# Two attention accumulators, and four PSUM banks shared in time, in a fused pooling-attention and mixture-of-depths kernel

## The chip, the core and the metric

The kernel runs on one core of a Trainium2 chip. The metric is the device time of one execution in microseconds (us), lower is better. The engines are called PE (TensorE, the matmuls), DVE (VectorE), ACT (ScalarE), POOL (GpSimd) and SP (SyncE, which here only issues DMAs). Each engine works through its own instructions in the order in which the program lists them, and waits on semaphores for the others. All arithmetic is fp32 unless said otherwise.

## What is computed

```python
# attention: B, H, S, D = 8, 8, 576, 64; keys and values are averaged over groups of 8 rows
k_p = k.reshape(B, H, Sp, pool, D).mean(axis=3)          # Sp = 72
v_p = v.reshape(B, H, Sp, pool, D).mean(axis=3)
scores = scale * np.matmul(q, k_p.transpose(0, 1, 3, 2))
attn = np.exp(scores - max); attn = attn / (attn.sum(-1) + 1e-09)
x = np.matmul(attn, v_p)                                  # to (B, S, 512)
# mixture of depths: 128 of 576 rows of each batch go through a small network
scores = np.einsum('bsd,d->bs', x, w_gate)
out = x.copy()
for b in range(B):
    top_idx = np.argpartition(-scores[b], capacity)[:capacity]   # capacity = 128
    xe = x[b, top_idx]
    ye = np.maximum(xe @ w1, 0.0) @ w2                    # 512 -> 1024 -> 512
    g = 1.0 / (1.0 + np.exp(-scores[b, top_idx]))
    out[b, top_idx] = x[b, top_idx] + g[:, None] * ye
```

## The kernel before

The kernel is one long program with its order written out by hand: nothing is rescheduled, and each engine executes its part of the list in that order. The names below are functions of the kernel; a line such as L232 is a line of it.

The 576 rows of a batch are cut into six chunks of 96 rows, so there are 48 chunks `a` in the whole program. Two chunks make a unit `u` (24 units, three a batch).

Attention, per unit and chunk:

- `pool_k` and `pool_v` add up groups of eight rows of k and v, on POOL for all batches but the first; `k_trans` and `q_trans` transpose on DVE; `gate_v` (L194) appends to the pooled v a column for the gate's score, beside a column of constants which gives the sum of the exponentials.
- `scores(u)` (L216) makes 16 matmuls, which use the PE array in four groups of 32 rows, into the PSUM tile `pS` (four banks). One ACT instruction of 72 x 1536 elements (L220) takes the exponential of all of it into `et`.
- `attend(a)` (L232) makes eight matmuls, one a head, into the PSUM tile `pA` (two banks, one buffer).
- `norm(a)` reads the sum of the exponentials and the gate's column from `pA` on ACT (L244, L245), inverts the sum on DVE (L247) and multiplies the rows by it into `xs` (L248).
- `store_x(u)` writes two chunks to the output in HBM; ACT's queue issues it.

The mixture of depths, for each batch after its attention, spread over the steps of the following batches:

- `score` adds the heads' gate scores (DVE), and POOL splits them into three bf16 numbers each. `row_bcast` (L293, L295) spreads the scores along rows with PE transposes and ACT copies, in two halves. `count` (L305 to L309) counts on DVE for each row how many have a higher score, `one_hot` (L316) makes a selection matrix of that, and `gather` (L323) multiplies it with indices and scores, whereupon POOL issues an indirect DMA that fetches the 128 chosen rows from the output in HBM (`xr`); it waits for the batch's stores.
- `gate` computes the sigmoid, `x_trans` (L346, L348) transposes the chosen rows, `hidden` (L358, L361) is the first product with its Relu, `finish` (L368, L373) the second, with the gate, the addition of the row, and an indirect DMA that scatters the rows to the output.

The PSUM of eight banks is divided like this: `pS` four, `pA` two, `pM` one (`row_bcast`, `gather`, `x_trans` and `hidden`, one after the other), `pF` one (`finish`).

The order comes from a main loop over chunks and a table of jobs. `at(a, slot, job)` puts a job into one of four slots of the step of chunk `a`; the loop runs slot 0, then `attend` and `norm` of the chunk, slot 1, in even steps `scores(u + 1)` and `q_trans(u + 2)`, and slots 2 and 3. The pieces of `hidden` and `finish` are spread over slots 1 and 2, so that they stand between `attend` and `scores` on PE:

```python
        for n, f in enumerate((0, 1, 2, 3, 4, 5, 8, 6, 7, 9, 10, 11, 12, 13, 14, 15)):
            c = (0, 0, 1, 1, 2, 2, 2, 3, 3, 3, 4, 4, 4, 5, 5, 5)[n]
            slot = (1, 2, 1, 2, 1, 2, 2, 1, 2, 2, 1, 2, 2, 1, 2, 2)[n]
            at(e + 8 + c, slot, *((hidden, b, f) if f < 8 else (finish, b, f - 8)))
```

At the start, k and q of batch 0 are loaded through SP's queue and v through ACT's. v has three buffers of half a batch each (`vraw`), k and q two each. At the end, a small check of the exponentials' sums sets a flag; a general path (not taken here) would follow if it were set.

Of the kernel before, what the change touches and what calls it, by code (L numbers as in the profile page):

```python
# [48 lines left out]
def direct_path(ctx, tc, q, k, v, moe_w_gate, moe_w1, moe_w2, moe_capacity, out, flag):  # L49
# [7 lines left out]

    nc = tc.nc

    B, H, S, D = q.shape  # L60
    POOLW = 8
# [24 lines left out]
    psum = ctx.enter_context(tc.tile_pool(name="psum", bufs=1, space=bass.MemoryType.PSUM))  # L86
# [14 lines left out]
    def load_v(b, g, eng):  # L101
        x = work.tile([SP, HG, POOLW, D], FT, name="vraw", bufs=3)
        VR[b, g] = x
        src = v[b, HG * g : HG * (g + 1)].rearrange("h (p t) d -> p h (t d)", t=POOLW)
        for lo, hi in ((0, 64), (64, SP)):
            eng.dma_start(out=x[lo:hi].rearrange("p h t d -> p h (t d)"), in_=src[lo:hi])

    load_k(0)
    load_v(0, 0, nc.scalar)
    load_q(0)  # L110
    load_v(0, 1, nc.scalar)
# [6 lines left out]
    eps = const.tile([C, 1], FT)  # L118
    nc.vector.memset(eps, 1e-9 * POOLW)
# [18 lines left out]
    zall = const.tile([C, B, NC, H], FT)  # L138
    cmp = const.tile([C, S], BF)
# [69 lines left out]
    def scores(u):  # L209
        b = u // NTH  # L210
        p = psum.tile([SP, 4, 4, 128], FT, name="pS")
        for s in range(2):
            for j in range(2):
                for i in range(4):
# [5 lines left out]
        nc.scalar.activation(ET[u].rearrange("p n g t -> p n t g"),  # L220
                             p.rearrange("p i n x -> p (i n) x")[:, :, 0:C].rearrange("p n (t g) -> p n t g", g=G),
                             AF.Exp, scale=exp_scale)
# [13 lines left out]
    def norm(a):  # L236
        b, c = divmod(a, NC)
        o = PA.pop(a)
        if c == 0:
# [3 lines left out]
        z = zall[:, b, c, :]  # L243
        nc.scalar.activation(z.rearrange("p (g n) -> p g n", g=2), o[:, :, :, D], AF.Identity, bias=eps)  # L244
        nc.scalar.copy(out=SS[b][:, c, :].rearrange("p (g n) -> p g n", g=2), in_=o[:, :, :, D + 1])  # L245
        rz = RZ[b][:, c, :]
# [4 lines left out]
                                op=OP.mult)  # L251

    SC, SR, CN, OH, XR, GV, XG, HT, PH, PF = ({} for _ in range(10))
# [11 lines left out]
    def store_x(u):  # L267
        b, th = divmod(u, NTH)
        c = slice(2 * th, 2 * th + 2)
        i = nc.scalar.dma_start(out=out[b].rearrange("(p c) d -> p c d", c=NC)[:, c, :], in_=XS[b][:, c, :])  # L270
        others(i, b, (scat, gath))
        store.setdefault(b, []).append(i)

    def score(b):
        nc.vector.tensor_tensor(out=SS[b], in0=SS[b], in1=RZ[b], op=OP.mult)
# [11 lines left out]
    def row_bcast(b, half):  # L287
# [3 lines left out]
        p = psum.tile([C, n, C], FT, name="pM")  # L291
# [27 lines left out]
    def gather(b):  # L319

        p = psum.tile([cap, 5], FT, name="pM")
# [21 lines left out]
    def x_trans(b):  # L343
        p = psum.tile([128, DB, cap], FT, name="pM")
# [5 lines left out]
    def hidden(b, f):  # L350

        if f == 0:
            HT[b] = work.tile([128, FB, cap], FT, name="ht")
        if f % 4 == 0:
            PH[b] = psum.tile([128, 4, cap], FT, name="pM")
        p = PH[b]
        for d in range(DB):
            nc.tensor.matmul(p[:, f % 4, :], w1[:, d, 128 * f : 128 * f + 128], XG[b][:, d, :],  # L358
                             start=(d == 0), stop=(d == DB - 1))
        if f % 4 == 3:  # L360
            nc.scalar.activation(HT[b][:, f - 3 : f + 1, :], p, AF.Relu)  # L361

    def finish(b, f):

        if f == 0:
            PF[b] = psum.tile([cap, DM], FT, name="pF")
        p = PF[b]
        nc.tensor.matmul(p, HT[b][:, f, :], w2[:, f, :], start=(f == 0), stop=(f == FB - 1))  # L368
        if f < FB - 1:
            return  # L370
        idx, g = GV[b]
        y = work.tile([cap, DM], FT, name="y")
        nc.vector.scalar_tensor_tensor(y, p, g, XR[b], op0=OP.mult, op1=OP.add)  # L373
        i = nc.gpsimd.indirect_dma_start(  # L374
            out=out_rows, out_offset=bass.IndirectOffsetOnAxis(ap=idx[:, :1], axis=0), in_=y, in_offset=None)
        others(i, b, (store, scat, gath))
        scat[b] = [i]
# [5 lines left out]
    def at(a, slot, *job):  # L383
        jobs.setdefault((a, slot), []).append(job)


    for u in range(NU):
        at(2 * u + 2, 1, store_x, u)
    for b in range(B):
        e = NC * (b + 1)  # L390
        last = b == B - 1
        at(e - 1, 3, score, b)
        at(e, 2, row_bcast, b, 0)
        at(e, 3, row_bcast, b, 1)
        for c in range(NC):
            at(e + (1 if last else (2, 2, 3, 3, 4, 5)[c]), 3, count, b, c)
        at(e + (2 if last else 5), 3, one_hot, b)
        at(e + (5 if last else 6), 3 if last else 1, gather, b)
        at(e + 7, 1, gate, b)
        at(e + 7, 3, x_trans, b)  # L400
        for n, f in enumerate((0, 1, 2, 3, 4, 5, 8, 6, 7, 9, 10, 11, 12, 13, 14, 15)):
            c = (0, 0, 1, 1, 2, 2, 2, 3, 3, 3, 4, 4, 4, 5, 5, 5)[n]
            slot = (1, 2, 1, 2, 1, 2, 2, 1, 2, 2, 1, 2, 2, 1, 2, 2)[n]
            at(e + 8 + c, slot, *((hidden, b, f) if f < 8 else (finish, b, f - 8)))
        if b + 1 < B:
            a = NC * b
            at(a, 0, pool_k, b + 1, nc.gpsimd)
            at(a + 1, 3, pool_v, b + 1, 0, nc.gpsimd)
            at(a + 2, 1, k_trans, b + 1)
            at(a + 3, 3, pool_v, b + 1, 1, nc.gpsimd)  # L410
            at(a + 4, 3, gate_v, b + 1, 0)
# [408 lines left out]
```

## Time and profile before

| what | value |
|---|---|
| median of 3 runs | 365.27 us (361.26 to 367.03) |
| the profiled execution | 366.8 us, span 364.9 us |
| mean granted clock of PE | 0.865 of full speed |
| busy: PE, DVE, POOL, ACT | 275.2, 177.9, 134.5, 104.9 us |
| DMA | 46.75 MB, mean 128 GB/s |

The span is the time from the first to the last instruction of the profiled execution; the 1.9 us beside it are the launch's. Busy time is the time in which an engine executes; the rest it waits, for a semaphore or for its next instruction. A PE instruction is shown twice (each fp32 matmul leaves two records), so that `attend` has 16 records and `scores` 32. The granted clock of PE is 1.00 or 0.50 in the trace.

### The profile page before, as it was taken

To read this page: it belongs to the slowest core of one execution; us is meant where nothing else is said; L and a number is where in the kernel's file an instruction comes from. 1 tells how busy PE (TensorE), PEld (TensorE's weight loads), DVE (VectorE), ACT (ScalarE), POOL (GpSimd) and SP (SyncE) were. 2 spreads that over 40 slices of the span, in tenths; PEclk is the share of its full clock that TensorE was granted. 3 is DMA by queue.
4 is the path that set the end of the run, shared out by engine and by line. 5 is a ranking of instruction groups with operands and counts; after the bars stand their busy time and mean duration, and the time that the engine had idled before them with its cause. 6 is when DMAs were issued, how large, how long until landed. Compare 5 with 4: busy or idle time off the path is not lost.

```text
span 364.9 us, 5869 instructions
## 1 busy us (share of the span) xinstructions
PE 275.2 (75%) x2306; PEld 216.3 (59%) x2306; DVE 177.9 (49%) x524; ACT 104.9 (29%) x169; POOL 134.5 (37%) x156
## 2 busy tenths in 40 slices
PE   0303777788658988969778989698879889989890
PEld 0203666576637875767557755686668669556650
DVE  3249244158423752594429723946294627563001
ACT  0310333422240444324314441432343244110100
POOL 1177501950359015660647064805390210121101
PEclk9999766655565998988999998969996999999996
DMA  7932999961781178306661686031121113210101
GB/s 272 268 58 54 372 353 304 321 140 44 208 249 50 44 195 247 94 15 151 224 158 31 141 295 142 0 110 46 38 65 43 46 29 93 66 60 11 48 0 39
DMA packets 12952, 46.75 MB, mean 128 GB/s; under 512 B 1324, under 2 KB 1324, under 8 KB 10868
## 3 DMA queue, kind: packets, MB, share of 16 engines
q1 hardware_dynamic: 8240, 31.33, 29.4%
q10 hardware_dynamic: 3396, 10.77, 10.0%
q0 software_dynamic: 1280, 4.20, 4.2%
q8 instruction: 20, 0.33, 0.4%
q14 instruction: 16, 0.13, 0.1%
HBM read 34.75 MB, written 11.53 MB: 127 GB/s over the span
## 4 chain that ended last, share of the span: by engine, by line
PE 44%; DVE 22%; DMA 16%; ACT 6%; issue 5%; POOL 4%; ACTq 1%; DVEq 0%; SPq 0%; POOLq 0%
PE pA L232 14%; PE pM L358 10%; PE pS L216 8%; DMA xr<-out_dram,idx 8%; PE pF L368 8%; DMA vraw<-in_v_dram 7%; DVE xs L248 4%; ACT et L220 4%; DVE cmp L309 3%; POOL kraw L169 2%; DVE cmp L305 2%; DVE qt L204 2%; DVE cmp L307 2%; DVE oh L316 2%; DVE kh L175 2%
## 5 line engine op out<-in xcount | busy, mean ns | idle before, releaser
L232 PE MATMUL pA<-vp,et 72*96 72x66 f32 x768 | 90.8, 281 | 47.7 <-DVE vp L194 24.6
L232 PEld LDWEIGHTS pA<-vp,et 72*96 72x96 f32 x768 | 86.3, 195 | 59.0 <-issue 28.5
L220 ACT ACTIVATE et<-pS 72x1536 f32<-72x1536 f32 x24 | 70.7, 2947 | 61.9 <-PE pS L216 61.9
L358 PE MATMUL pM<-xg,w 128*128 128x128 f32 x512 | 71.3, 292 | 2.8 <-ACT xg L348 1.5
L358 PEld LDWEIGHTS pM<-xg,w 128*128 128x128 f32 x512 | 65.0, 203 | 8.7 <-issue 5.0
L368 PE MATMUL pF<-w,ht 128*128 128x512 f32 x128 | 65.2, 632 | 0.0
L247 DVE RECIPROCAL rz<-zall 96x8 f32<-96x8 f32 x48 | 9.5, 198 | 113.9 <-ACT zall L244 112.4
L216 PE MATMUL pS<-qt,kt 32*72 32x192 f32 x768 | 52.4, 428 | 12.0 <-DVE qt L204 12.0
L216 PEld LDWEIGHTS pS<-qt,kt 32*72 32x72 f32 x768 | 36.5, 184 | 19.4 <-DVE qt L204 12.0
L281 POOL CAST auxb<-sc 96x6 bf16<-96x6 f32 x8 | 1.6, 199 | 121.0 <-DVE sc L277 105.0
L186 POOL TENSOR_TENSOR vraw<-vraw 72x1024 f32<-72x1024 f32 x15 | 35.5, 2368 | 19.7 <-DMA vraw<-in_v_dram 19.6
L244 ACT ACTIVATE zall<-pA,eps 96x8 f32<-96x8 f32 x48 | 12.2, 254 | 93.8 <-PE pA L232 93.8
L248 DVE TENSOR_TENSOR xs<-pA,rz 96x512 f32<-96x512 f32 x48 | 33.0, 687 | 6.7 <-DVE rz L247 0.9
L368 PEld LDWEIGHTS pF<-w,ht 128*128 128x128 f32 x128 | 22.9, 200 | 17.9 <-issue 17.9
L307 DVE TENSOR_SCALAR_CACHE_REDUCE cmp<-sr,sc 96x576 bf16<-96x576 f32 (+5 forms) x48 | 26.6, 554 | 0.0
L204 DVE STREAM_TRANSPOSE qt<-qraw 128x768 f32<-128x768 f32 x24 | 23.2, 966 | 0.9 <-DMA qraw<-in_q_dram 0.9
L374 POOL DMA_INDIRECT out_dram<-y,idx x8 | 8.5, 1064 | 40.1 <-DVE y L373 22.0
L309 DVE SCALAR_TENSOR_TENSOR cmp<-sr,sc,before 96x96 bf16<-96x96 f32 x48 | 21.9, 456 | 0.3
L373 DVE SCALAR_TENSOR_TENSOR y<-pF,g,xr 128x512 f32<-128x512 f32 x8 | 6.0, 750 | 29.5 <-PE pF L368 29.5
L305 DVE TENSOR_SCALAR_CACHE_REDUCE cmp<-sr,sc 96x96 bf16<-96x96 f32 (+4 forms) x40 | 20.0, 499 | 0.7
L187 POOL TENSOR_TENSOR vraw<-vraw 72x512 f32<-72x512 f32 x15 | 19.1, 1277 | 1.2
L361 ACT ACTIVATE ht<-pM 128x512 f32<-128x512 f32 x16 | 9.6, 597 | 33.6 <-PE pM L358 33.6
(68 smaller groups left out, 182.4 us busy)
## 6 DMA issues: line engine op xcount, KB each, us to landing
kraw<-in_k_dram SPq DMA_DIRECT2D x8, 1152.0 KB
qraw<-in_q_dram SPq DMA_DIRECT2D x8, 1152.0 KB, 6.7
out_dram<-xs ACTq DMA_DIRECT2D x24, 384.0 KB, 3.0
vraw<-in_v_dram SPq DMA_DIRECT2D x14, 512.0 KB, 9.0
w<-in_moe_w_dram SPq DMA_DIRECT2D x2, 2048.0 KB, 27.3
vraw<-in_v_dram ACTq DMA_DIRECT2D x2, 512.0 KB, 19.9
vraw<-in_v_dram SPq DMA_DIRECT2D x14, 64.0 KB
wg<-in_moe_w_gate_dram ACTq DMA_DIRECT2D x1, 144.0 KB
```

The costliest lines, as they stand in the source:

```text
L186: eng.tensor_tensor(out=x[:, :, 0:4, :], in0=x[:, :, 0:4, :], in1=x[:, :, 4:8, :], op=OP.add)
L187: eng.tensor_tensor(out=x[:, :, 0:2, :], in0=x[:, :, 0:2, :], in1=x[:, :, 2:4, :], op=OP.add)
L204: nc.vector.transpose(out=QT[u].rearrange("p cc j t c -> p t (cc j) c"), in_=QR[b].rearrange("p (t c) d -> p t (c d)", c=NC)[:, :, 2 * D * ...
L216: nc.tensor.matmul(p[:, i, 2 * s : 2 * s + 2, 0:C], KT[b][r, j, s, :], QT[u][r, :, j, :, G * s : G * s + G], start=(j == 0), stop=(j == 1))
L220: nc.scalar.activation(ET[u].rearrange("p n g t -> p n t g"), p.rearrange("p i n x -> p (i n) x")[:, :, 0:C].rearrange("p n (t g) -> p n t ...
L232: nc.tensor.matmul(p[:, g, E * n : E * n + E], ET[u][:, 2 * h + cc].rearrange("p g t -> p (g t)"), VP[b][:, h, :], start=True, stop=True)
L248: nc.vector.tensor_tensor(out=XS[b][:, c, :].rearrange("p (g n d) -> p g n d", g=2, d=D), in0=o[:, :, :, 0:D], in1=rz.rearrange("p (g n on ...
L305: nc.vector.tensor_scalar(cmp[:, 0 : c * C], row[:, 0 : c * C], s, None, op0=OP.is_ge, op1=OP.add, accum_out=CN[b][:, c, 0:1])
L307: nc.vector.tensor_scalar(cmp[:, c * C : S], row[:, c * C : S], s, None, op0=OP.is_gt, op1=OP.add, accum_out=CN[b][:, c, 1:2])
L309: nc.vector.scalar_tensor_tensor(cmp[:, 0:C], row[:, c * C : c * C + C], s, before, op0=OP.is_equal, op1=OP.mult, accum_out=CN[b][:, c, 2:3])
L358: nc.tensor.matmul(p[:, f % 4, :], w1[:, d, 128 * f : 128 * f + 128], XG[b][:, d, :], start=(d == 0), stop=(d == DB - 1))
L368: nc.tensor.matmul(p, HT[b][:, f, :], w2[:, f, :], start=(f == 0), stop=(f == FB - 1))
```

## The change

- `pA` gets two buffers of two banks each. The other four banks are one tile, `shared`, allocated once. `scores` uses all four banks of it, and all jobs of the mixture of depths use one bank each: `row_bcast` banks 1 and 3, `gather` bank 2, `x_trans` bank 0, `hidden` in three parts (three, three and two of the eight blocks of 128 hidden units) banks 0, 1 and 0, `finish` in three parts banks 1, 0 and 2.
- The exponential of a unit is four ACT instructions, one for each bank.
- `norm` reads `pA` on DVE alone: the sum with its small constant, the reciprocal, the rows, and the gate's column already multiplied by the reciprocal.
- `finish` computes 176, 176 and 160 of the 512 columns in its parts, each over all eight blocks; ACT multiplies a part by the gate, POOL adds the row.
- The main loop runs over units. A step is `attend` and `norm` of the first chunk, `scores(u + 1)`, `attend` and `norm` of the second chunk, `q_trans(u + 2)`, and then the jobs of slots 3 to 7, so that all matmuls of the mixture of depths stand behind the second `attend` of their step.
- All loads go through SP's queue, v has four buffers, and the loads of batch 1 and of w1 are issued before any work; the stores move from ACT's queue to SP's. `scores(1)` is moved ahead of the first `attend`. A first exponential of one column loads ACT's table early.

```diff
-    psum = ctx.enter_context(tc.tile_pool(name="psum", bufs=1, space=bass.MemoryType.PSUM))
+    psum = ctx.enter_context(tc.tile_pool(name="psum", bufs=2, space=bass.MemoryType.PSUM))
...
+    shared = psum.tile([128, 4, 512], FT, name="shared", bufs=1)
...
     def scores(u):
-        p = psum.tile([SP, 4, 4, 128], FT, name="pS")
+        p = shared[:SP].rearrange("p i (n x) -> p i n x", n=4)
...
-        nc.scalar.activation(ET[u].rearrange("p n g t -> p n t g"),
-                             p.rearrange("p i n x -> p (i n) x")[:, :, 0:C].rearrange("p n (t g) -> p n t g", g=G),
-                             AF.Exp, scale=exp_scale)
+        for i in range(4):
+            nc.scalar.activation(ET[u][:, 4 * i : 4 * i + 4].rearrange("p n g t -> p n t g"),
+                                 p[:, i, :, 0:C].rearrange("p n (t g) -> p n t g", g=G), AF.Exp, scale=exp_scale)
...
-        nc.scalar.activation(z.rearrange("p (g n) -> p g n", g=2), o[:, :, :, D], AF.Identity, bias=eps)
-        nc.scalar.copy(out=SS[b][:, c, :].rearrange("p (g n) -> p g n", g=2), in_=o[:, :, :, D + 1])
+        nc.vector.tensor_scalar(z.rearrange("p (g n) -> p g n", g=2), o[:, :, :, D], 1e-9 * POOLW, None, op0=OP.add)
         nc.vector.reciprocal(rz, z)
         nc.vector.tensor_tensor(out=XS[b][:, c, :] ...
+        nc.vector.tensor_tensor(out=SS[b][:, c, :].rearrange("p (g n) -> p g n", g=2),
+                                in0=o[:, :, :, D + 1], in1=rz.rearrange("p (g n) -> p g n", g=2), op=OP.mult)
...
-        i = nc.scalar.dma_start(out=out[b].rearrange("(p c) d -> p c d", c=NC)[:, c, :], in_=XS[b][:, c, :])
+        i = nc.sync.dma_start(out=out[b].rearrange("(p c) d -> p c d", c=NC)[:, c, :], in_=XS[b][:, c, :])
...
     def row_bcast(b, half):
-        p = psum.tile([C, n, C], FT, name="pM")
+        p = shared[:C, 2 * half + 1, 0 : n * C].rearrange("p (c i) -> p c i", c=n)
...
-    def hidden(b, f):
+    def hidden(b, part, bank):
+        fs = range(FB)[3 * part : 3 * part + 3]
+        p = shared[:, bank, 0 : len(fs) * cap].rearrange("p (f i) -> p f i", i=cap)
+        for n, f in enumerate(fs):
+            for d in range(DB):
+                nc.tensor.matmul(p[:, n, :], w1[:, d, 128 * f : 128 * f + 128], XG[b][:, d, :],
+                                 start=(d == 0), stop=(d == DB - 1))
+        nc.scalar.activation(HT[b][:, fs[0] : fs[-1] + 1, :], p, AF.Relu)
...
-    def finish(b, f):
+    def finish(b, part, bank):
+        c = slice(176 * part, min(176 * part + 176, DM))
+        p = shared[:cap, bank, 0 : c.stop - c.start]
+        for f in range(FB):
+            nc.tensor.matmul(p, HT[b][:, f, :], w2[:, f, c], start=(f == 0), stop=(f == FB - 1))
+        nc.scalar.activation(Y[b][:, c], p, AF.Copy, scale=g)
+        nc.gpsimd.tensor_tensor(out=Y[b][:, c], in0=Y[b][:, c], in1=XR[b][:, c], op=OP.add)
...
+        w = NTH * (b + 1)
+        at(w - 1, 7, score, b)
+        at(w, 4, row_bcast, b, 0)
+        at(w, 6, row_bcast, b, 1)
+        for c in range(NC):
+            at(w + (0 if last else (0, 0, 1, 1, 1, 2)[c]), 7, count, b, c)
+        at(w + (0 if last else 2), 7, one_hot, b)
+        at(w + 2, 7, gather, b)
+        at(w + 3, 2, gate, b)
+        at(w + 3, 7, x_trans, b)
+        at(w + 4, 3, hidden, b, 0, 0)
+        at(w + 4, 5, hidden, b, 1, 1)
+        at(w + 5, 3, hidden, b, 2, 0)
+        at(w + 5, 5, finish, b, 0, 1)
+        at(w + 6, 3, finish, b, 1, 0)
+        at(w + 6, 5, finish, b, 2, 2)
...
+    for u in range(NU + 7):
+        run(u, 0)
+        if u < NU:
+            attend(2 * u)
+            norm(2 * u)
+        run(u, 1)
+        if 0 < u < NU - 1:
+            scores(u + 1)
+        run(u, 2)
+        if u < NU:
+            attend(2 * u + 1)
+            norm(2 * u + 1)
+        if u + 2 < NU:
+            q_trans(u + 2)
+        for slot in range(3, 8):
+            run(u, slot)
```

## The prediction

> **What bounds the kernel now.** I read the page first: busy shares, clock, chain.
>
> ```profile
> PE 275.2 (75%) x2306; PEld 216.3 (59%) x2306; DVE 177.9 (49%) x524; ACT 104.9 (29%) x169; POOL 134.5 (37%) x156
> ...
> PEclk9999766655565998988999998969996999999996
> ...
> PE 44%; DVE 22%; DMA 16%; ACT 6%; issue 5%; POOL 4%; ACTq 1%; DVEq 0%; SPq 0%; POOLq 0%
> ```
>
> TensorE (PE) is busiest and has the most of the chain, but not half of it: DVE and DMA end much of the rest. In slices 4 to 12 the granted clock is about half. Next, the waits: waiter, releaser, total us, times, longest.
>
> ```profile
> PE pA L232 <- DVE vp L194: 24.6, 7, 18.1
> ...
> PE pA L232 <- DVE xs L248: 20.6, 9, 3.3
> ...
> PE pM L293 <- ACT sr L295: 11.8, 8, 2.7
> ```
>
> The first is mostly the start (18.1 us, the pooled v). The second is the single accumulator pA: `attend` waits until DVE has divided the chunk before. The third is `row_bcast` half 1 waiting for pM. Then PE's timeline in the middle (start, us, records; `[...]` is idle time before):
>
> ```profile
> 224.17 1.50 PE L232 MATMUL pA<-vp,et 72*96 72x66 f32 x16
> 225.50 1.11 PE L358 MATMUL pM<-xg,w 128*128 128x128 f32 x8
> 226.54 1.54 PE L216 MATMUL pS<-qt,kt 32*72 32x192 f32 x32
> 228.01 1.16 PE L358 MATMUL pM<-xg,w 128*128 128x128 f32 x8
> 229.00 1.50 PE L232 MATMUL pA<-vp,et 72*96 72x66 f32 x16
> 230.34 2.00 PE L358 MATMUL pM<-xg,w 128*128 128x128 f32 x16
> 235.61 2.54 PE L232 MATMUL pA<-vp,et 72*96 72x66 f32 x16 [3.27 <-DVE xs L248]
> ```
>
> From start to next start, at full clock: an `attend` 1.33, a `scores` 1.47, and (205.87 to 207.71, same view) 16 hidden records 1.84, so 0.115 each. `scores` (L216) is followed at once by a piece of `hidden` (L358): the exponential of pS runs beside it, because `hidden` has its own bank. Keep that in mind. Last, the windows (length, then busy us of PE, PEld, DVE, ACT, POOL; then clock):
>
> ```profile
> 195.03:198.44 3.41, 1.91 (x17) 1.72 (x16) 3.21 (x12) 1.44 (x4) 3.25 (x3) 1.00 0.00 0
> 232.57:235.99 3.42, 0.38 (x4) 0.39 (x5) 3.25 (x13) 0.41 (x1) 3.19 (x4) 1.00 0.00 0
> 235.99:239.40 3.41, 3.41 (x21) 3.41 (x21) 2.64 (x12) 0.32 (x2) 0.06 (x1) 0.50 0.13 38
> ```
>
> 3.4 us with almost no matmul and the clock is 0.50 afterwards (until 242.8); 1.8 us of idle beside 1.9 us of `hidden` does not do it.
>
> **The change, part by part.** I work in steps u of two chunks (three a batch), in three stretches: to the start of step 7, where the first `hidden` comes (before: 111.9 us); steps 7 to 23 (before: 111.9 to 314.3, so 202 for 17); the tail (50.6).
>
> *Waits that the shared tile adds.* By name the four banks are independent. In the built program they are not: the first matmul of a `hidden` group in bank 0 waits for the ScalarE count that the fourth exponential of its step raises, `hidden` part 1 (bank 1) for the Relu of part 0 (bank 0), `row_bcast` half 1 (bank 3) for the copy of the `finish` part ahead of it. Each write to any bank waits for the last reader of any bank. So in every step all mixture-of-depths matmuls queue on PE behind four exponentials, and each group behind the copy of the one before. The prices:
>
> ```profile
> L220 ACT ACTIVATE et<-pS 72x1536 f32<-72x1536 f32 x24 | 70.7, 2947 | 61.9 <-PE pS L216 61.9
> ...
> L361 ACT ACTIVATE ht<-pM 128x512 f32<-128x512 f32 x16 | 9.6, 597 | 33.6 <-PE pM L358 33.6
> ...
> L295 ACT COPY sr<-pM 96x288 f32<-96x288 f32 x16 | 6.7, 418 | 8.0 <-PE pM L293 8.0
> ```
>
> From the last two: 0.80 ns per element and 0.19 us fixed. The exponential streams 2.947 - 0.19 = 2.76. Split in four it costs at least 2.95 (no fixed cost repeated) and at most 2.76 + 4 x 0.19 = 3.52. At 35.80 us the 0.26 us activation of L244 is followed by L245 already at 35.96, an overlap of 0.10; so 0.09 per extra part, 3.22. The Trainium skill (ScalarE: Activation LUTs, What ACT_TABLE_LOAD costs) gives 186 ns plus 0.833 ns per element and an overlap of about 93 ns back to back. By its rate all four would take some 1.6 us; the trace's 2947 ns contradicts that rate here, and only the overlap agrees.
>
> With 0.12 for two semaphore hops (a 0.42 copy leaves PE idle 0.53 at 319.26), `hidden` or `finish` starts 3.34 after `scores`; the second `attend` covers 1.33. Stall per step: 2.01. Copies: Relu of 384 elements 0.50, of 256 0.39, sr 0.42, a `finish` part 0.43 (176 elements, and 0.10 for the scale operand, as L244's 254 ns against L245's 152); with hops 0.64, 0.53, 0.54, 0.57.
>
> *Matmuls.* `finish` goes from 8 matmuls of 512 columns to 24 of 176, 176 and 160. A record of L368 takes 0.43, of 128 columns 0.115, so 0.154 and 0.141: 16 x (0.154 + 0.154 + 0.141) = 7.2 against 6.9 a batch.
>
> *A batch of steps 7 to 23.* Each step: 4.13 attention plus 2.01 = 6.14.
> Step with `hidden` 0 and 1: 6.14 + 2 x 2.76 + 0.64 = 12.3.
> With `hidden` 2, `finish` 0, gather: 6.14 + 1.84 + 0.53 + 2.46 + 0.57 + 0.30 = 11.8.
> With `finish` 1, 2, both `row_bcast` (0.45 each) and `x_trans` (0.63): 6.14 + 2.46 + 0.57 + 0.45 + 0.54 + 2.26 + 0.57 + 0.45 + 0.54 + 0.63 = 14.6, and 0.4 of what remains of the wait for vp (1.02 at 250.44): 15.0.
> Sum 39.1 a batch; six, six and five of them 219.8. A group that starts anew costs 0.12 more (eight records 1.04, not 0.92): seven a batch, 4.5 in all. So **224**, where the kernel before needs 202.
>
> *What is taken away there.* The 1.8 to 3.3 us waits on xs: with two accumulators DVE may be a chunk late, and its 22.2 us a batch (177.9 / 8), with twelve more small operations of 0.2 (L247's 198 ns) 24.6, fit in 39. The gather's transfer (5 to 8 us) is now covered by 13.9 us of PE work. Both are already left out of the 39.1. POOL has room (134.5 / 8 = 16.8 us a batch, plus three adds of about 0.5 by L188's 745 ns for 256 elements). So has SP: stores now queue there behind loads, but the loads' buffers are free a batch ahead, and the gather, which waits for a batch's stores, comes two steps after the last of them. I cost these at nothing; a store that came late by more than that would delay `x_trans` by its lateness.
>
> *Clock.* Before, 34 us of the 202 ran at 0.50. The new low stretch per step, an `attend` plus 2.01 of waiting, is 3.34 us, just what the windows above punish if it falls in one. I take the same 34 us; PE is 74% busy, so 34 x 0.5 x 0.74 = **13**. Bounds: 0, and twice as much, 25. The skill (TensorE: Matmul & The Clock Gate, HAM oscillation) warns of idle gaps beyond about 3.4 us. By it alone gaps of 2 us cost nothing; the trace (2.2 us busy in 215.5 to 218.9, yet 0.50 after) is stricter.
>
> *Start.* Loads of batch 0 in one queue: v half 1 lands near 15 (at 270 GB/s, 3.7 MB from 2 us) instead of 23.1, and is pooled with POOL idle: 2.9 us rather than 9.3. `scores(0)` ends at 16, exponentials 19.3, `scores(1)` 22.2, two cold `attend` (2.83 each) 28: step 1 starts there, before at 42.5. Steps 1 and 2: 5.2 at full clock, 8.5 at half; 7 each, 42. Step 3: 9, 51. Then DVE decides up to the gather: 3.1 + 10.5 + 6.6 = 20.2 (counts, k and q transposes, four-operation norms of 1.28), 71. Transfer and transpose 11 to 12: step 7 at **83** (77 to 88), 29 earlier.
>
> *Tail.* `finish` of batch 5 to `x_trans` of batch 6 9.7; `hidden` 9.2; `finish` 0 and gather 3.8; `finish` 1, 2 5.9; `x_trans` 1.4; `hidden` 9.2; `finish` 8.3: 47.4, and 9.5 to the end (9.2 after the last L368 before, 0.3 for copy and add in place of L373): **57**, 6 more.
>
> Sum of spans: 83 + 224 + 13 + 57 = 377, against 364.9; with the 1.9 us around it 379, against the profiled execution's 366.8. The median of the runs is 1.5 below that execution: **378**. Measured, 2% of 365.27 about tells a change: 358.0 and 372.6.
>
> **Rivals.**
> *The clock holds.* If in steps 7 to 23 no 3.4 us window holds an `attend` and the wait together, the 13 goes: **365**, not slower; with the start at 77 and exponentials of 2.95 (17 x 0.27 = 4.6 less) 354. It decides once fewer than some 15 us of these steps run at 0.50 (15 x 0.37 = 6, and the sum is at 371). For it: 195.03 above. Against: 34 us even before.
> *Colder still.* Without `hidden` between attention pieces, every second step loses a window: 13 becomes 25 and the start 88: **395**.
> *The banks are independent on the chip.* Then the stalls of 10 us a batch fall to 2 and the kernel takes about **323**. Against it stand the built program's waits.
>
> **How the numbers follow.** Main case 0.56 (its own range 366 to 390), clock holds 0.22, colder 0.17, independent banks 0.05. Below 358.0: the last and a quarter of the second, 0.11; within 2%: the rest of the second (0.16) and a fifth of the first (0.11), 0.27; slower 0.62. The range 360 to 397 leaves out 0.1 on each side.
>
> **What would show it.** PE waits on the exponentials (L228) of about 2 us in each of steps 7 to 23, about 35 us in all, and further ones on ACT copies; no waits on xs; step 7 at 83; `hidden` rows starting 3.3 after `scores` ends; more slices at half clock. I am wrong if `hidden` starts right after the second `attend`, if steps 7 to 23 take under 210, or if step 7 comes after 95.

## The result, and the profile after

The changed kernel takes 394.32 us (median of 4 runs, 388.17 to 398.48) beside 365.28 us for the kernel before: the ratio is 1.070, with a 95% interval from 1.052 to 1.088. It is slower. The profiled execution took 390.54 us, with a span of 388.8 us. (Here and below the medians hold all executions, while the ratios leave out those that are over 1.5% longer than the fastest of the same kernel.)

First the page of the changed kernel: busy shares, clock, chain, and the exponentials' group.

```profile
PE 294.7 (76%) x2562; PEld 261.5 (67%) x2562; DVE 184.6 (47%) x604; ACT 103.9 (27%) x178; POOL 146.4 (38%) x180
...
PEclk9999999999999898888999889889998999989997
...
PE 65%; ACT 21%; DVE 4%; issue 3%; DMA 3%; SPq 1%; POOL 0%; POOLq 0%; ACTq 0%; DVEq 0%
...
L228 ACT ACTIVATE et<-shared 72x384 f32<-72x384 f32 x96 | 70.4, 890 | 111.0 <-PE shared L223 111.0
```

The chain says what has happened: DVE fell from 22% of it to 4%, DMA from 16% to 3%, and ACT rose from 6% to 21%. ACT has no more work than before (103.9 us, 104.9 before); PE now waits for it. PE is busy for 294.7 us, 19.5 more than before, although the arithmetic is the same.

Where the time went is read from windows over the three stretches of the prediction (length, then busy us and instructions of PE, PEld, DVE, ACT, POOL; then clock, DMA share, GB/s):

```profile
0.00:94.60 94.60, 64.10 (x502) 54.14 (x503) 49.13 (x147) 26.53 (x39) 44.48 (x51) 1.00 0.88 246
94.60:329.70 235.10, 189.77 (x1783) 170.78 (x1782) 125.45 (x411) 69.05 (x119) 90.29 (x108) 0.93 0.32 94
329.70:388.80 59.10, 40.79 (x278) 36.54 (x278) 10.03 (x48) 8.32 (x20) 11.64 (x23) 0.93 0.08 24
```

| stretch | before | predicted | after |
|---|---|---|---|
| start to step 7 | 111.9 | 83 | 94.6 |
| steps 7 to 23 | 202.4 | 237 (224 + 13 for the clock) | 235.1 |
| tail | 50.6 | 57 | 59.1 |

So the start gains 17.3 us, the middle loses 32.7 and the tail 8.5. For the middle, the same window of the kernel before reads:

```profile
111.90:314.30 202.40, 177.67 (x1603) 142.07 (x1603) 114.60 (x348) 70.34 (x116) 81.21 (x92) 0.91 0.37 103
```

PE was idle for 24.7 us of it and is now for 45.3, and it is busy for 12.1 us longer. The idle time is in the list of PE's waits within 94.6 to 329.7 us (waiter, releaser, total us, times, longest):

```profile
PE shared L364 <- ACT et L228: 16.8, 11, 1.6
PE shared L376 <- ACT g L345: 8.0, 5, 1.6
PE shared L299 <- ACT y L377: 4.9, 10, 0.5
...
PE pA L239 <- DVE vp L201: 0.4, 1, 0.4
```

The first two rows are the waits behind the four exponentials. (In the second the profile names `gate`'s small exponential g. It stands right behind the four on ACT, at 298.11 to 298.32 us for example, so it is the ACT instruction that ended last; the waiting `finish` part does not read g, and the length, 1.6, is that of the waits behind the four.) They are 16 waits and 24.8 us. The third row, with five more like it, are groups of mixture-of-depths matmuls that wait for the copy of the group before: 19.5 us in all (4.9, twice 3.5, 2.8, and twice 2.4). The wait on xs that cost 20.6 us before is gone. One step on PE's timeline shows both kinds:

```profile
269.02 1.54 PE L223 MATMUL shared<-qt,kt 32*72 32x192 f32 x32
270.49 1.57 PE L239 MATMUL pA<-vp,et 72*96 72x66 f32 x16
273.69 2.94 PE L364 MATMUL shared<-xg,w 128*128 128x128 f32 x24 [1.63 <-ACT et L228]
277.21 2.94 PE L364 MATMUL shared<-xg,w 128*128 128x128 f32 x24 [0.58 <-ACT ht L366]
...
298.37 4.33 PE L376 MATMUL shared<-w,ht 128*128 128x176 f32 x16 [1.57 <-ACT g L345]
```

`hidden` part 0 writes bank 0 and could have started when the first exponential had read that bank. It starts at 273.69. ACT's timeline of the same moment has

```profile
270.69 2.95 ACT L228 ACTIVATE et<-shared 72x384 f32<-72x384 f32 x4 [2.31 <-PE shared L223]
```

which ends at 273.64: the start waits for the fourth exponential. Part 1 writes bank 1, which nobody uses then, and waits 0.58 us for the Relu that reads bank 0. The last line is a `finish` part largely at half rate: 4.33 us, where the same 16 records take 2.65 us at 288.58.

### The profile page after: what moved, and what is told of

The parts are those of the page before. It is cut to its first block, busy times and chain, and to the rows that moved or that the text cites. A ratio compares the mean times of both kernels' runs of the same rounds, so it can differ in the third digit from the quotient of the medians.

```text
span 388.8 us, 6486 instructions
## 1 busy us (share of the span) xinstructions
PE 294.7 (76%) x2562; PEld 261.5 (67%) x2562; DVE 184.6 (47%) x604; ACT 103.9 (27%) x178; POOL 146.4 (38%) x180
## 4 chain that ended last, share of the span: by engine, by line
PE 65%; ACT 21%; DVE 4%; issue 3%; DMA 3%; SPq 1%; POOL 0%; POOLq 0%; ACTq 0%; DVEq 0%
PE shared L364 18%; PE shared L376 18%; ACT et L228 14%; PE pA L239 13%; PE shared L223 13%; DMA qraw<-in_q_dram 3%; ACT y L377 2%; PE shared L299 2%; ACT ht L366 2%; ACT sr L301 2%; PE shared L352 1%; DVE qt L211 1%; PE shared L329 1%; DVE vp L201 1%; DVE kh L182 1%
## 5 line engine op out<-in xcount | busy, mean ns | idle before, releaser
L228 ACT ACTIVATE et<-shared 72x384 f32<-72x384 f32 x96 | 70.4, 890 | 111.0 <-PE shared L223 111.0
L239 PEld LDWEIGHTS pA<-vp,et 72*96 72x96 f32 x768 | 88.2, 202 | 12.8 <-issue 11.3
L364 PE MATMUL shared<-xg,w 128*128 128x128 f32 x512 | 69.5, 296 | 24.0 <-ACT et L228 16.8
L376 PE MATMUL shared<-w,ht 128*128 128x176 f32 (+1 forms) x384 | 71.2, 345 | 17.0 <-ACT g L345 8.0
L364 PEld LDWEIGHTS shared<-xg,w 128*128 128x128 f32 x512 | 64.5, 207 | 28.2 <-ACT et L228 18.3
L376 PEld LDWEIGHTS shared<-w,ht 128*128 128x128 f32 x384 | 64.7, 213 | 21.6 <-ACT g L345 8.7
L378 POOL TENSOR_TENSOR y<-y,xr 128x176 f32<-128x176 f32 (+1 forms) x24 | 13.0, 543 | 171.0 <-ACT y L377 171.0
L223 PE MATMUL shared<-qt,kt 32*72 32x192 f32 x768 | 49.9, 411 | 21.0 <-DVE qt L211 15.6
L223 PEld LDWEIGHTS shared<-qt,kt 32*72 32x72 f32 x768 | 35.0, 175 | 27.7 <-DVE qt L211 15.6
L366 ACT ACTIVATE ht<-shared 128x384 f32<-128x384 f32 (+1 forms) x24 | 10.9, 455 | 73.6 <-PE shared L364 73.6
L311 DVE TENSOR_SCALAR_CACHE_REDUCE cmp<-sr,sc 96x96 bf16<-96x96 f32 (+4 forms) x40 | 20.2, 504 | 0.9
L176 POOL TENSOR_TENSOR kraw<-kraw 128x1152 f32<-128x1152 f32 x7 | 18.3, 2621 | 5.6 <-DMA kraw<-in_k_dram 5.6
```

What stands on the lines that cost most here:

```text
L223: nc.tensor.matmul(p[:, i, 2 * s : 2 * s + 2, 0:C], KT[b][r, j, s, :], QT[u][r, :, j, :, G * s : G * s + G], start=(j == 0), stop=(j == 1))
L228: nc.scalar.activation(ET[u][:, 4 * i : 4 * i + 4].rearrange("p n g t -> p n t g"), p[:, i, :, 0:C].rearrange("p n (t g) -> p n t g", g=G) ...
L239: nc.tensor.matmul(p[:, g, E * n : E * n + E], ET[u][:, 2 * h + cc].rearrange("p g t -> p (g t)"), VP[b][:, h, :], start=True, stop=True)
L311: nc.vector.tensor_scalar(cmp[:, 0 : c * C], row[:, 0 : c * C], s, None, op0=OP.is_ge, op1=OP.add, accum_out=CN[b][:, c, 0:1])
L364: nc.tensor.matmul(p[:, n, :], w1[:, d, 128 * f : 128 * f + 128], XG[b][:, d, :], start=(d == 0), stop=(d == DB - 1))
L376: nc.tensor.matmul(p, HT[b][:, f, :], w2[:, f, c], start=(f == 0), stop=(f == FB - 1))
```

## The experiments

The theory to test: the loss comes from `shared` being one tile, so that a write to any bank waits for the last reader of any bank. The rivals: the exponential in four pieces, the new order with all mixture-of-depths work behind the second `attend`, or the clock. A second question is why the start came 11.6 us later than predicted.

**One tile for each bank.** Four tiles of one bank in place of one tile of four. The same instructions on the same banks in the same order; only the guard is finer.

```diff
-    shared = psum.tile([128, 4, 512], FT, name="shared", bufs=1)
+    shared = [psum.tile([128, 512], FT, name=f"bank{i}", bufs=1) for i in range(4)]
...
```

> The changed kernel with one edit: the four banks are four tiles of one bank each, so that a write to one bank waits only for the last reader of that bank. Theory A (the waits that the single tile adds cost the time): in steps 7 to 23 the profile of the changed kernel shows PE waiting 1.6 us behind the exponentials in every step and 0.5 to 0.6 behind a copy six times a batch; 3 x 1.6 + 4 x 0.48 + 0.58 + 0.59 = 7.9 us a batch, 45 us in 17 steps, and some 5 in the tail: 335 to 350 us, and the PE rows 'shared <- ACT' fall from some 50 us to under 10. Theory B (the order is at fault: all mixture-of-depths work behind the second attend, with the clock falling in the low stretch before it): the waits only move to DVE and to the half clock, 380 us or more.

Measured: 324.6 us (323.68 to 327.65), ratio 0.887 (0.880 to 0.894). Against the changed kernel that is 70 us less for one line of allocation (the other lines of the edit only index the four tiles), and 10 us below the range of theory A, which had counted the waits and left the half rate as it was. Its waits between step 7 and step 24 (89.2 to 277 us) are a list of one line, and the window of that stretch follows:

```profile
PE bank L329 <- DVE oh L322: 10.3, 5, 2.4
```

```profile
89.19:277.06 187.87, 177.00 (x1784) 166.03 (x1783) 130.65 (x416) 68.08 (x118) 91.65 (x108) 0.90 0.42 119
```

On PE's timeline `hidden` now follows the second `attend` at once, at 196.28 us, while ACT works on the exponentials of that step from 195.01 to 198.01; its two parts are one run of 48 records:

```profile
194.87 1.57 PE L239 MATMUL pA<-vp,et 72*96 72x66 f32 x16
196.28 5.58 PE L364 MATMUL bank<-xg,w 128*128 128x128 f32 x48
...
213.01 0.32 PE L329 MATMUL bank<-auxb,oh 96*128 96x5 bf16 x6 [2.45 <-DVE oh L322]
...
216.00 2.85 PE L223 MATMUL bank<-qt,kt 32*72 32x192 f32 x32
```

The stretch fell by 47.2 us, from 235.1 to 187.9. PE's idle time in it fell by 34.4 (45.3 to 10.9), its busy time by 12.8 (189.8 to 177.0): fewer restarts of groups, and fewer matmuls at half rate. The rest of the 70 us is in the tail (59.1 to 45.3) and the start (94.6 to 89.2). So the waits are the tile's. The busy time fell together with them; how firmly PE's rate hangs on such waits is taken up under the warming kernels. The Trainium skill (PSUM — Partial Sum Buffer, PSUM bank collisions raise a hardware error) asks for a guard by bank, with a quarter of the partitions as the finest grain, and says that accesses of two engines to different banks run clean. The trace agrees (`hidden` at 196.28, above): bank by bank is enough, and the guard of the changed kernel, over four banks, was coarser than what that section asks.

The last lines show what is left: in four of the five batches of the list the gather waits 2.45 us for one_hot (0.54 in the first), and the `attend` and `scores` behind it take 2.87 and 2.85 us instead of 1.50 and 1.54.

**One exponential again**, all else as in the changed kernel.

```diff
-        for i in range(4):
-            nc.scalar.activation(ET[u][:, 4 * i : 4 * i + 4]...
+        nc.scalar.activation(ET[u].rearrange("p n g t -> p n t g"), ...
```

> The changed kernel with the exponential of a unit as one instruction of 1536 elements again, the shared tile as it is. The four parts together last 2.95 us in the profile (18.48 to 21.43), as the one did before. Theory A: since every write to the tile waits for the last of the four, nothing is lost by one: within 1% of the changed kernel. Theory B says the same here. Against both: if the pairs of heads that start after the first part matter, in the steps without mixture-of-depths work, 1 to 2 us a step are lost in steps 1 to 6, 6 to 12 us in all.

Measured: 395.6 us (386.47 to 402.52), ratio 1.078 (1.069 to 1.088): the changed kernel's time, as expected. In this kernel the single exponential has a mean of 2934 ns (L227, 24 of them), and the four take 2.95 us. Splitting costs nothing, and under a common tile it brings nothing.

**One accumulator** in the changed kernel.

```diff
-        p = psum.tile([C, 2, 512], FT, name="pA")
+        p = psum.tile([C, 2, 512], FT, name="pA", bufs=1)
```

> The changed kernel with one buffer of the accumulator pA (two banks stay empty). Theory A: in this order DVE has the matmuls of the mixture of depths to catch up, so the second accumulator saves only about 1 us a batch in steps 7 to 23, and what the scores do not cover of the 1.3 us of a norm in steps 1 to 6: 0 to 12 us more than the changed kernel. Rival: the accumulator is what the change lives on, and the waits of 1.8 to 3.3 us on xs of the kernel before come back, 3 a batch and more: 20 us more.

Measured: 420.1 us (416.29 to 424.15), ratio 1.136 (1.128 to 1.144), 26 more than with two: the rival's 20 and more, not theory A's 0 to 12. Its page and its waits:

```profile
PE 326.1 (77%) x2562; PEld 289.9 (69%) x2562; DVE 181.6 (43%) x604; ACT 103.8 (25%) x178; POOL 146.0 (35%) x180
```

```profile
PE pA L239 <- DVE ss L257: 15.3, 10, 2.7
```

The wait for DVE is back with 15.3 us, but the waits behind the exponentials fall by 10.6 (in the same list from 24.8 to 11.3 + 2.9 = 14.2), for they overlap. What remains is PE's busy time, 31 us longer for the same instructions, where its idle time is only 2 us longer (96.2 and 94.1). (The profiled execution took 424.1 us, 8 more than the shortest of the six; some of the 31 is that.) So the loss is in PE's rate far more than in the length of the waits. That the waits lower the rate is inferred from the two coming together.

**The new order with the old banks.** `scores` has four banks of its own, `pA` one buffer, the mixture of depths two one-bank tiles (banks 0 and 2 are one, 1 and 3 the other).

```diff
-    shared = psum.tile([128, 4, 512], FT, name="shared", bufs=1)
+    shared = [psum.tile([128, 512], FT, name=f"bank{i}", bufs=1) for i in range(2)]
...
-        p = shared[:SP].rearrange("p i (n x) -> p i n x", n=4)
+        p = psum.tile([SP, 4, 4, 128], FT, name="pS", bufs=1)
...
-        p = psum.tile([C, 2, 512], FT, name="pA")
+        p = psum.tile([C, 2, 512], FT, name="pA", bufs=1)
...
```

> The changed kernel's order and jobs with the banks divided as before: the scores in four banks of their own, one accumulator of two banks, and two tiles of one bank each, in turn, for the mixture of depths. Theory A: hidden and finish wait neither for exponentials nor for the copy just ahead, so nearly all of the 45 us come back; the single accumulator takes 0 to 12 of them: 340 to 360 us. Theory B (the order): 380 us or more.

Measured: 352.7 us (351.61 to 354.81), ratio 0.962 (0.956 to 0.969). That is within theory A's range. The order is not at fault; with the loads, the other norm and the finer pieces of work it gains some 12 us even on the old division of banks. Its first wait is the old one:

```profile
PE pA L239 <- DVE ss L257: 23.8, 13, 3.6
```

Three kernels now apportion the change by medians: order, loads, norm and finer pieces 365.3 to 352.7 (-12.6); the second accumulator, with bank-by-bank guards, 352.7 to 324.6 (-28.1); the common tile 324.6 to 394.3 (+69.7).

**v of batch 0 on ACT's queue** as before, in the changed kernel.

```diff
-    load_v(0, 0)
+    load_v(0, 0, nc.scalar)
     load_q(0)
-    load_v(0, 1)
+    load_v(0, 1, nc.scalar)
...
```

> The changed kernel with the v of batch 0 loaded through ACT's queue again, beside k and q on SP's; all else as changed. Theory A (the single load queue is what brings the start forward, as forecast: v half 1 is not delayed by the loads of batch 1): v half 1 lands at about 23 us instead of about 15, step 1 comes 8 to 12 us later and so do step 7 and the end: 398 to 406 us. Rival (the start is set by k, q and PE's half rate, and the pooled v is ready in time either way, or the other edits of the start brought the gain): 390 to 396, no difference that can be measured.

Measured: 401.9 us (399.18 to 408.32), ratio 1.101 (1.082 to 1.120), within theory A's range. PE's timeline:

```profile
11.87 2.85 PE L223 MATMUL shared<-qt,kt 32*72 32x192 f32 x32 [11.87 <-DVE qt L211]
...
25.52 1.55 PE L239 MATMUL pA<-vp,et 72*96 72x66 f32 x8 [3.53 <-DVE vp L201]
34.86 6.67 PE L239 MATMUL pA<-vp,et 72*96 72x66 f32 x40 [7.79 <-DVE vp L201]
```

And the changed kernel's own start on PE:

```profile
15.56 2.85 PE L223 MATMUL shared<-qt,kt 32*72 32x192 f32 x32 [15.56 <-DVE qt L211]
...
24.26 7.95 PE L239 MATMUL pA<-vp,et 72*96 72x66 f32 x48
...
49.65 2.80 PE L239 MATMUL pA<-vp,et 72*96 72x66 f32 x16 [2.56 <-DVE sc L283]
...
82.42 0.32 PE L329 MATMUL shared<-auxb,oh 96*128 96x5 bf16 x6 [4.76 <-DVE oh L322]
```

One queue has its price and its gain. q lands behind half of v (on DVE, `q_trans` starts at 14.53 after a wait for q's transfer), so the first scores start 3.7 us later (15.56, not 11.87). But v is in time: the 3.5 and 7.8 us of waiting for it are gone, and step 7 comes at 94.6 instead of 102.66. The single queue is worth 8 us of the start's 17.3; what brought the other 9 was not separated.

**Early one_hot, with one-bank tiles.** The last count and one_hot go ahead of the second norm of their step.

```diff
-            at(w + (0 if last else (0, 0, 1, 1, 1, 2)[c]), 7, count, b, c)
-        at(w + (0 if last else 2), 7, one_hot, b)
+            at(w + (0 if last else (0, 0, 1, 1, 1, 2)[c]), 2 if c == 5 and not last else 7, count, b, c)
+        at(w + (0 if last else 2), 7 if last else 2, one_hot, b)
```

> Four one-bank tiles, and in the step after a batch's second one the last count and one_hot stand ahead of scores' second attend on DVE (before its norm), not behind it. In the kernel with one-bank tiles PE waits for one_hot before the gather 2.45 us in each of six batches, and the attention behind it runs at half rate for some 2 us more. Theory A (that wait is the last one on PE's path and feeds the half clock): the wait goes, 6 x 2.45 = 15 us, and up to 6 x 1.5 = 9 more for the clock: 300 to 310 us. Rival (DVE is the bound of that step, busy for 188 us of 322): the norm comes later by the 2.5 us of the moved work, PE waits for pA in place of one_hot, and the time stays at 318 to 325.

Measured: 324.6 us (323.5 to 326.11), ratio 0.897 (0.886 to 0.908). No gain: the rival that another DVE wait takes its place was right in the effect, though not in the place. PE's timeline behind a gather, then a line of DVE's for the first batch in the same kernel:

```profile
140.99 1.54 PE L239 MATMUL pA<-vp,et 72*96 72x66 f32 x16 [2.07 <-DVE g L335]
142.46 2.85 PE L223 MATMUL bank<-qt,kt 32*72 32x192 f32 x32
```

```profile
78.26 0.38 DVE L201 TENSOR_REDUCE vp<-vraw 72x4 f32<-72x256 f32 x1
```

From step 7 on the gather waits no more (1.34 us are left at the first one, in the start), but the first `attend` of the next batch waits 2.07 us, and the profile names L335, the DVE instruction that ended last ahead of it. Behind the first gather that `attend` starts at 78.78. L201 ends at 78.64: it is `gate_v` half 0, which writes the gate's column of the v that this `attend` reads, and it stands behind the norm that one_hot has pushed back. That is a reading; the next kernel puts it to the test.

**gate_v ahead too.**

```diff
-            at(u + 2, 3, gate_v, b + 1, 0)
-            at(u + 2, 7, gate_v, b + 1, 1)
+            at(u + 2, 0, gate_v, b + 1, 0)
+            at(u + 2, 2, gate_v, b + 1, 1)
```

> The kernel with one-bank tiles and the early one_hot, and the two gate_v of the next batch moved ahead too (half 0 before the step's first norm, half 1 between one_hot and the second norm). In the kernel with the early one_hot alone, PE waited 2.06 us in each of five batches before the first attend of a batch; I read it as gate_v half 0, which stands on DVE behind norm and q_trans: it ends at 78.64 us and that attend starts at 78.78. Theory A: with gate_v ahead the wait is gone, 5 x 2.06 = 10 us, and part of the half-rate stretch behind it (scores 2.85 instead of 1.5 after it): 303 to 313 us. Rival (the attend waits for the norm or the gather's sums, not for gate_v, or the next DVE work takes its place): 319 to 326.

Measured: 307.9 us (304.49 to 312.44), ratio 0.845 (0.839 to 0.851): the fastest by its median, 57 us under the kernel before, and within theory A's range. Its window of steps 7 to 23:

```profile
88.22:257.17 168.95, 164.34 (x1784) 155.75 (x1783) 124.05 (x410) 68.22 (x118) 89.49 (x107) 0.97 0.44 129
```

PE is busy for 164.3 of 169.0 us (the largest wait left there is 2.7 us in all for the gather's rows, xr), and runs at half rate only at the stretch's start and around 152 us. The wait of 2.07 us ahead of a batch's first `attend` is gone, so the reading was right. Compared with the kernel with one-bank tiles alone, idle time fell by 6.3 us and busy time by 12.7; whether the busy time fell because of this edit is taken up below.

**Warming PE.** Four kernels add matmuls whose results nobody reads: 18 (or 48) of 128 x 128 by 128 columns ahead of the first scores, and two of 96 rows ahead of each of the first 14 `attend`.

```diff
+    for i in range(18):
+        nc.tensor.matmul(shared[i % 4][:, 0:128], diff, diff, start=True, stop=True)
     scores(0)
...
+        if a < 14:
+            for g in range(2):
+                nc.tensor.matmul(p[:, g, 384:512], diff[:, 0:C], diff, start=True, stop=True)
```

With one-bank tiles:

> Four one-bank tiles, and matmuls whose results nobody reads: 18 of 128 x 128 by 128 columns before the first scores, where PE is idle until 15.6 us, and two such (of 96 rows) ahead of each of the first 14 attends. Theory A (the start takes longer than forecast because its matmuls run at half rate: an attend takes 2.83 us there, 1.5 later): the attends and scores of steps 0 to 6 run at full rate, 14 x 1.3 + 6 x 1.4 = 27 us of matmul time less the extra 28 x 0.23 = 6, and where DVE does not wait for something else step 7 comes at 75 to 83 instead of 89.2: 308 to 318 us. Rival 1 (attention alone falls back to half rate at once, whatever went ahead): the extra matmuls cost 28 x 0.46 = 13 and step 7 comes at 92 to 102: 327 to 337. Rival 2 (DVE, the pooling and the loads set the start): rate full, but step 7 not before 87: 321 to 326.

With the early one_hot:

> Both of the edits of the two other kernels together (one-bank tiles, early one_hot, extra matmuls in the start). Theory A of both: the gains add, 290 to 303 us. If one_hot's move or the warm start brings nothing: 303 to 318.

With the early gate_v as well, and then with 48:

> The same with the 18 early matmuls and the two ahead of each of the first 14 attends, whose results nobody reads. With the early one_hot these brought 324.6 to 312.2, with one-bank tiles alone nothing. Theory A (the clock holds only where no wait is left in the start; each wait removed makes the warm matmuls worth more): 294 to 304 us. Rival (they shift the phase of the clock by chance): no better than the kernel without them.

> The same with 48 early matmuls instead of 18. With 18, PE is busy from 1.1 to 7.6 us and idle until the first scores at 15.8, and scores and the first attends still run at half rate. Theory A (that idle gap is why): with 48 the burst lasts till about 14.5, scores(0) takes 1.5 instead of 2.85 and the first attends 1.5; step 1 comes some 5 us earlier: 289 to 299 us. Rival (attention falls back to half rate within a few us all the same): within 2 us of the kernel with 18.

Measured, with the same kernel without these matmuls behind it: 325.4 (319.49 to 329.11) beside 324.6; 312.2 (309.08 to 322.57) beside 324.6; 316.4 (310.06 to 317.91) beside 307.9; and 310.3 (302.04 to 316.84) with 48. With 18, one of three is better, one no different and one worse; with 48 it is no better either, and the executions of one kernel differ by up to 15 us: no general gain. Theory A's range was missed each time.

Only in the second pair do the times stand apart (309.08 to 322.57 beside 323.5 to 326.11 us), and there the traces say where the difference lies. Step 7 comes at 88.87 us with the extra matmuls and at 88.56 without: the start gained nothing. From there to the end of step 23 the two kernels have the same instructions. These are the windows, first without and then with the matmuls in the start:

```profile
88.56:276.24 187.68, 178.75 (x1784) 167.85 (x1783) 129.57 (x416) 68.24 (x118) 92.08 (x108) 0.89 0.41 118
88.87:261.93 173.06, 164.20 (x1783) 155.35 (x1783) 129.26 (x416) 68.11 (x118) 91.66 (x108) 0.97 0.44 128
```

PE is idle for 8.9 us in both, with the same four waits of some 2.07 us ahead of a batch's first `attend`, and it is busy for 14.6 us less. Without the extra matmuls its rate falls behind all four waits (140.99 and 142.46 above are one); with them behind one, and three look like this:

```profile
235.21 1.54 PE L242 MATMUL pA<-vp,et 72*96 72x66 f32 x16 [2.08 <-DVE g L338]
236.68 1.54 PE L223 MATMUL bank<-qt,kt 32*72 32x192 f32 x32
```

So the same wait in the same code costs PE's rate in one kernel and not in the other. The gain is no warm start; it fits the rival of a shift by chance, and what decides is not shown. It also bears on the early gate_v, whose stretch is 18.7 us shorter than with the early one_hot alone (187.68 to 168.95): 4.3 us of that are idle time and 14.4 are PE's rate, and here the rate came back with the waits still in place. So the 4.3 us are the edit's; the 14.4 cannot be put down to it with certainty.

For the start itself, the trace of the kernel with 48 (an execution of 316.84 us, the longest of its four) has

```profile
1.12 13.64 PE L446 MATMUL bank<-diff 128*128 128x128 f32 x96 [1.12 <-POOL diff L127]
17.15 2.85 PE L223 MATMUL bank<-qt,kt 32*72 32x192 f32 x32 [2.39 <-DVE qt L211]
```

96 records in 13.64 us are 0.142 each: with 0.115 at full rate and 0.230 at half, some 23 ran at half (5 us) and the rest at full. After 2.39 us of idle time the scores take 2.85, half rate. PE is almost never idle until 45 us and yet stays at half until about 58 us, although extra matmuls fill a third of the time (1.11 us beside an `attend` of 2.72). In the kernel with the early one_hot and 18, the same sequence is back at full rate at 36.6 us (`attend` in 1.50 at 37.12 and 38.92). So the burst does warm PE, the rate was gone after 2.4 us of idle time, and attention with extra matmuls brought it back after some 20 us in one execution and some 40 in another. The theory that the start needs only 48 early matmuls fell in this execution; a burst without any gap before the first scores was not run.

## Why the prediction was right, and where it was off

*The direction and the cause* were right: each write to `shared` waits for the last reader of any bank. One-bank tiles take that away and 70 us with it. The rival "the banks are independent on the chip" was priced at 323; a kernel in which the program lets them be independent takes 324.6. As a forecast of the changed kernel it was wrong, but its price was right, in part by luck: its sum starts from step 7 at 83 us, and even that kernel reaches it only at 89.2.

*The sum.* The span is 388.8, not 377: 11.6 too little for the start, 2.2 too much for steps 7 to 23, 2.1 too little for the tail. The median lies 3.8 above the profiled execution here, not 1.5 below it as for the kernel before. Hence 394.3 beside 378, near the upper end of the range. Of the cases laid out, "colder still" (chance 0.17, 395 us) is nearest, in its 25 us for the clock as well as in the total, though its stalls were too long and its start, 88, too early.

*Stall behind the exponentials: 2.01 predicted, 1.6 measured.* The step that missed is "so 0.09 per extra part, 3.22". Four exponentials of 890 ns would be 3.56 in a row; together they take 2.95, the lower of my two bounds, so 0.2 us of each following one lies beside the one before. The 0.12 for hops was too much as well: `hidden` starts 0.05 us behind the last exponential. The Trainium skill (ScalarE: Activation LUTs, What ACT_TABLE_LOAD costs) has an overlap of about 93 ns back to back; (3.56 - 2.95) / 3 = 0.20 here, more than double. By that page's figures (186 ns plus 0.833 ns per element) four parts would take 4 x 0.506 - 3 x 0.093 = 1.74 us, an estimate, not the 1.6 of the prediction; neither is near 2.95. I also counted 17 stalls; there are 16, since step 23 has no scores. Together 34.2 predicted and 24.8 measured.

*Gaps behind copies*: 0.64, 0.53, 0.54 and 0.57 predicted (a copy and 0.12, added up, are 0.62, 0.51, 0.54 and 0.55); the trace has 0.58 and 0.47 behind the Relus, 0.48 behind sr, 0.50 to 0.59 behind a `finish` part. 6 x 0.64 + 6 x 1.10 + 5 x 2.22 = 21.5 predicted in this stretch, 19.5 measured.

*The clock: 13 predicted, about 25 measured, which was the upper bound.* My 224.3 less the stalls (34.2), the copies (21.5), the vp wait (2.0) and a scores too many (1.5) leaves 165.1 us of matmuls at full rate. The fastest kernel is busy for 164.3 there (4.5 of it lost to half rate, and about 4.5 less than mine for groups that start anew). The changed kernel is busy for 189.8, so 24.7 more; the kernel before was busy for 177.7 with nearly the same work. "I take the same 34 us" failed: half rate costs about twice what it did. Behind 9 of the 16 waits for exponentials the next group runs at half rate in whole or in part (298.37), behind 7 at full rate (273.69). That the waits and the copy gaps bring it about is argued, not shown one by one; with one-bank tiles the waits and 12.8 us of busy time went together. This error and the two above cancel: -9.4 - 2.0 - 1.6 (vp, 0.4 measured) - 1.5 + 0.6 (idle time with no named releaser) + 11.7 = -2.2. That steps 7 to 23 came within 1% is in part luck.

*The start: step 7 at 94.6, not 83.* Step 1 starts at 24.26 + 2 x 2.65 = 29.6 instead of 28: q lands behind v half 0, for which I had allowed 1.1 us (`scores(0)` ending at 16, where it ended at 14.9 before); it took 3.5 (18.4), and with v on ACT's queue the first scores come 3.7 us earlier. Steps 1 and 2 took 20.1 instead of 14, since everything in them ran at half rate, with waits for kt (1.18) and, through DVE, of 2.56 at 49.65. Step 3 took 10.4 instead of 9, the stretch to the gather 22.4 instead of 20.2, and from there to step 7 12.2 instead of 11 to 12. The term that failed is "5.2 at full clock, 8.5 at half; 7 each": a mean, where the clock row of the kernel before is at about half from slice 4 to slice 12, all of this stretch. Why attention in the start runs mostly at half rate is open. It does not always: the kernel before has an `attend` of 1.57 us at 38.26.

*The tail*, 59.1 for 57: a `hidden` part largely at half rate (339.33, 4.57 us instead of 2.94) makes up most of the difference.

*What I said the profile would show.* No waits on xs: right. Waits on exponentials of about 2 us and 35 in all: right in kind, 1.6 and 24.8. `hidden` 3.3 us after scores: 273.69 - 270.56 = 3.1. Step 7 at 83: wrong, and at 94.6 just short of the 95 that I had set as a sign of being wrong. More slices at half clock: not in the page's clock row, which shows no 5 at all; only the matmuls' durations show the half rate.

## What to carry to other kernels

Before banks are shared in time, look at what the program guards: a tile over several banks may be guarded as one, and then a split reader or a second bank buys nothing, while a tile for each bank costs nothing. When a wait is taken away, follow the engine's queue to the instruction that is late next (here one_hot, then gate_v), since the first edit alone brought 0. And price a wait on PE as idle time and, as a range, as the half rate that may follow it: with the same waits of 2.07 us, 8.9 us of idle time in all, PE was busy for 14.6 us longer in one kernel than in another, for the same work. Before an edit is credited with a gain, look whether idle time or rate has changed.

## What the runs showed of the hardware

- PE's rate can fall after short waits. Idle stretches of 2.4 us (before the first scores of the kernel with 48 early matmuls, and before the gather with one-bank tiles) are followed by matmuls at half rate (scores 2.85 instead of 1.54). The Trainium skill (TensorE: Matmul & The Clock Gate, HAM oscillation) warns of idle gaps above about 3.4 us. The gaps here are shorter.
- The length of a wait does not decide it. Behind waits of 2.07 us ahead of the same `attend` the rate fell four times of four with the early one_hot, and once of four in the same code with extra matmuls in the start.
- PE's rate does not always rise with activity. From 17 to 45 us PE was almost without a gap in the kernel with 48 early matmuls and stayed at half, while the burst of full-size matmuls had brought it up after some 5 us. What the clock responds to, these runs do not settle.
- The clock column can mislead. The changed kernel's window 0 to 94.6 us shows 1.00 and its scores there take 2.85 us; with one-bank tiles the same scores take 2.85 us, and the window 0 to 89.19 us shows 0.74. The durations are the safer witness.
- The time of an ACT instruction in a row of its kind is no sum of means: 890 ns each, 2.95 us for four.
